# Running the two units of a quad together, array mode by array mode, in a retention and adapter kernel

## The chip, the core and the metric

The kernel runs on one core of one Trainium2 chip. The metric is the device time of one execution in microseconds (us). The profiles were taken by the hardware profiler during one execution.

## What is computed

The reference is a retention layer (attention without a softmax and with an exponential decay) whose output goes through a mixture of eight low-rank adapters, of which each token takes its best two. Everything is float32, with B = 8 sequences, H = 8 heads, S = 576 positions and 64 elements a head.

```python
scores = scale * q @ k.T                       # per sequence and head
Dmat   = where(i >= j, gamma[h] ** (i - j), 0) # causal decay
x      = (scores * Dmat) @ v                   # (8, 8, 576, 64)
x      = x.transpose(0, 2, 1, 3).reshape(4608, 512)
logits = x @ w_gate                            # 8 experts
w      = softmax of the two largest logits
out    = x + sum over the two experts e:  w_e * (x @ A[e]) @ B[e]   # rank 16
```

## The kernel before

Positions are cut into four full chunks of 128 and a last one of 64. A **quad** is one chunk of four sequences; its q, k and v arrive in three loads of 1 MB each. A **unit** is two sequences of a quad, so a quad has two units. There are 16 full units, numbered 0 to 15, and two units of the half chunk, 16 and 17. Quad n holds units 2n and 2n+1. Each unit passes eleven stages. The diff and the prediction call them by their letters:

| stage | engine | what it does | TensorE rows x columns |
|---|---|---|---|
| T | TensorE, then ScalarE or VectorE | transposes q (16 matmuls) and k (16), copies them out of PSUM | 64 x 128 |
| S | TensorE, VectorE | scores, 8 matmuls for each of two sequences, then the mask multiply into rt | 64 x 128 |
| Q | TensorE | state of earlier chunks times q, into px | 64 x 64 |
| U | TensorE, VectorE, GpSimd | state update, k times v, into pu, then P | 128 x 64 |
| R | TensorE, VectorE | rt times v, added into px, then the scaling into xT | 128 x 64 |
| B | TensorE | transposes xT back to tokens, into po | 64 x 128 |
| Z | TensorE, VectorE | x times A and the gate, into pz, then the two best logits | 128 x 128 |
| V | ScalarE | sigmoid of the logit difference | |
| W | VectorE | mixing weights, and zc = z times weight | |
| X | TensorE, ScalarE | transposes zc, copies it to zT | 128 x 128 |
| Y | TensorE, ScalarE | adds zT times B into po, copies po to osb, and a store follows | 128 x 128 |

The column on the right is the part of the array that each matmul of the stage addresses, which follows from the partitions of its operands. This document calls it the array mode. In the half chunk S, Q and R use 64 x 64.

Program order is kept on every engine by hand. The main loop handles one unit a turn:

```python
def issue(n):                      # the loads of quad n, all on the SyncE queue
    tl = [iop.tile([128, QUAD, H, Dh], FP32, tag=tag, name=tag) for tag in ("q32", "k32", "v32")]   # 3 buffers each
    ...
for t in range(NU):
    if units[t][2] == 0:           # first unit of a quad
        issue(quads.index(units[t][:2]) + 2)      # two quads ahead
    ... # (t = 0, 1, 2: a written-out start)
    if is_full(t):
        stage_S(t, (0,))
        stage_V(t - 1)
        stage_T(t + 1, ("qT",))
        stage_S(t, (1,))
        stage_W(t - 1)
        stage_T(t + 1, ("kT",))
        stage_B(t - 1)
        if units[t][0] > 0:
            stage_Q(t)
        ...
        stage_U(t)
        scale_k(t + 1)             # GpSimd scales k in place, U needs it
        ...
        stage_R(t)
        stage_X(t - 1)
        stage_Z(t)
        stage_Y(t - 1)
        continue
    ... # (the half chunk: units 16 and 17, one after the other)
```

PSUM banks come from a list of eight: a stage takes the bank that has been free longest in program order, and gives it back when the copy out of it has been put into the program.

Of the kernel before, what the change touches and what calls it, by code (L numbers as in the profile page):

```python
# [18 lines left out]
def kernel(  # L19
# [180 lines left out]
    def issue(n):  # L200
        if n >= len(quads):
            return
        c, qd = quads[n]
        first = n == 0
        tl = [
            iop.tile([128, QUAD, H, Dh], FP32, tag=tag, name=tag) for tag in ("q32", "k32", "v32")
        ]
        if c == NFULL:
            if qd > 0:
                return  # L210
            for src, dst in zip((q, k, v), tl):
                for g in range(2):
                    nc.sync.dma_start(
                        out=dst[64 * g : 64 * g + 64].rearrange("p s h d -> p (s h) d"),
                        in_=src[HALF * g : HALF * g + HALF, :, C * c : C * c + L, :].rearrange(
                            "s h j d -> j (s h) d"
                        ),
                    )
            for u in range(2):
                nat[(c, u, 0)] = [x[:, 2 * u : 2 * u + 2] for x in tl]  # L220
            return

        def load(n, lo, hi):
            nc.sync.dma_start(
                out=tl[n][:, lo:hi].rearrange("p b h d -> p (b h) d"),
                in_=(q, k, v)[n][
                    QUAD * qd + lo : QUAD * qd + hi, :, C * c : C * c + C, :
                ].rearrange("b h j d -> j (b h) d"),
            )

        if first:
            for lo in (0, 2):
                for n in range(3):
                    if n == 2 and lo == 0:
                        load_A()
                    load(n, lo, lo + 2)
        else:
            for n in range(3):
                load(n, 0, 4)
        for sl in range(2):  # L240
            nat[(c, qd, sl)] = [x[:, 2 * sl : 2 * sl + 2] for x in tl]
# [23 lines left out]
                op=ALU.mult,  # L265
            )

    def stage_T(t, names=("qT", "kT")):

        s = st.setdefault(t, {})  # L270
        for nm in names:
            src = nat[units[t]][0 if nm == "qT" else 1]
            dst = s[nm] = wk.tile([128, 2, HP, C], FP32, tag=nm, name=nm)
            ps = [bank([128, HP, 2, L], f"p{nm}") for _ in range(2)]
            for hp in range(HP):
                for b in range(2):
                    for g in range(2):
                        mm(
                            ps[g][:, hp, b, :],
                            lhsT=src[rows(g), b, 2 * hp : 2 * hp + 2, :],  # L280
                            rhs=id64[rows(g), :],
                            is_transpose=True,
                            start=True,
                            stop=True,
                        )
            for g in range(2):
                if is_full(t):
                    o = dst[:, :, :, rows(g)].rearrange("p b a i -> p a b i")
                else:
                    o = dst[:, g].rearrange("p a (b i) -> p a b i", b=2)  # L290
                if t == 0 and nm == "kT":
                    for b in range(2):
                        x = dst[:, b, :, rows(g)]
                        if g == 1:
                            vec("tensor_copy", out=x, in_=ps[g][:, :, b])
                        else:
                            act("copy", out=x, in_=ps[g][:, :, b])
                elif t < 2 and nm == "qT" or t < 3 and nm == "kT" and g == 1:
                    vec("tensor_copy", out=o, in_=ps[g])
                else:  # L300
                    act("copy", out=o, in_=ps[g])
            done(*ps)
# [99 lines left out]
    def stage_R(t):  # L402
# [5 lines left out]
        if is_full(t):  # L408
            for b in range(2):
                for hp in range(HP):  # L410
                    for ho in range(2):
                        h = 2 * hp + ho
                        mm(
                            px[b][rows(ho ^ b), hp, :],
                            lhsT=v32[:, b, h, :],
                            rhs=rt[(b, ho)][:, hp, :],
                            start=(c == 0 and hp == 0),
                            stop=True,
                            skip_group_check=True,
                        )  # L420
                xt = mo.tile([128, HP, C], FP32, tag="xT", name="xT", bufs=6)
                vec("tensor_tensor", out=xt, in0=px[b], in1=asc[b], op=ALU.mult)
                s["xT"].append(xt)
            done(*px)
            return
# [10 lines left out]
                            skip_group_check=True,  # L436
                        )
        for x in range(2):
            xt = mo.tile([128, HP, C], FP32, tag="xT", name="xT", bufs=6)
            vec("tensor_tensor",   # L440
                out=xt.rearrange("p a (y i) -> p a y i", y=2),
                in0=px[x].rearrange("p a (y i) -> p a y i", y=2),
                in1=asc[x][:, :, 0:L].unsqueeze(2).broadcast_to((128, HP, 2, L)),
                op=ALU.mult,
            )
            s["xT"].append(xt)
# [19 lines left out]

    BOTH = (0, 1)

    def stage_X(t, gs=BOTH):
        s = st[t]  # L470
        n = len(gs)
        pzt = bank([128, n, 128], "pzt", FP16)
        for y, g in enumerate(gs):
            mm(
                pzt[:, y, :], lhsT=s["zc"][g], rhs=ident16,
                is_transpose=True, start=True, stop=True,
            )
        zt = mo.tile([128, n, 128], FP16, tag=f"zT{n}", name="zT")
        act("copy", out=zt, in_=pzt)
        done(pzt)  # L480
        for y, g in enumerate(gs):
            s.setdefault("zT", {})[g] = zt[:, y, :]

    def stage_Z(t, gs=BOTH):
        s = st[t]
# [38 lines left out]
    def stage_W(t, gs=BOTH):  # L524
# [3 lines left out]
            stage_V(t, gs)  # L528
        lg, m8, ns, pz, sg = s.pop(("route", gs))
        cm = mo.tile([128, n, E], FP32, tag=f"cm{n}", name="cm")  # L530
        zc = mo.tile([128, n, ER], FP16, tag=f"zc{n}", name="zc")
        for y in range(n):
            vec(
                "scalar_tensor_tensor",
# [78 lines left out]
    for t in range(NU):  # L613
        if units[t][2] == 0:
            issue(quads.index(units[t][:2]) + 2)
        if t == 0:
# [13 lines left out]
            stage_Q(0)  # L630
            stage_R(0)
            stage_T(1, ("qT",))
            stage_T(1, ("kT",))
            scale_k(1)
            stage_Z(0)
            stage_S(1)
# [3 lines left out]
            stage_R(1)  # L640
            stage_T(2, ("qT",))
            stage_B(0)
            stage_X(0)
            stage_Z(1)
            stage_Y(0, spread=True)
            stage_T(2, ("kT",))
            scale_k(2)
            for ho in range(2):
                gp.tensor_tensor(
                    out=maskh[ho], in0=trih.unsqueeze(1).broadcast_to((128, HP, L)),  # L650
                    in1=heads(1, ho, L), op=ALU.mult,
                )
            continue
        if t == 1:
            continue
        if t == NU - 1:
            break
        if t == 2:
            stage_T(3, ("qT",))
            stage_B(1)  # L660
            stage_V(1)
            stage_S(2)
            stage_W(1)
            stage_T(3, ("kT",))
            stage_U(2)
            stage_Q(2)
            scale_k(3)
            stage_R(2)
            stage_X(1)
            stage_Z(2)  # L670
            stage_Y(1)
            continue
        if is_full(t):
            stage_S(t, (0,))
            stage_V(t - 1)
            stage_T(t + 1, ("qT",))
            stage_S(t, (1,))
            stage_W(t - 1)
            stage_T(t + 1, ("kT",))
            stage_B(t - 1)  # L680
            if units[t][0] > 0:
                stage_Q(t)
            if not is_full(t + 1):
                stage_S(t + 1)
                stage_Q(t + 1)
            stage_U(t)
            scale_k(t + 1)
            if units[t][0] == 0:
                stage_Q(t)
            stage_R(t)  # L690
            stage_X(t - 1)
            stage_Z(t)
            stage_Y(t - 1)
            continue

        stage_W(t - 1)
        stage_T(t + 1)
        stage_B(t - 1)
        stage_R(t)
        stage_Q(t + 1)  # L700
        stage_X(t - 1)
        stage_Z(t)
        stage_W(t)
        stage_Y(t - 1)
        stage_S(t + 1)
        stage_B(t)
        stage_X(t)
        stage_R(t + 1)
        stage_Y(t)
        for g in range(2):  # L710
            stage_Z(t + 1, (g,))
            stage_W(t + 1, (g,))
        stage_B(t + 1)
        for g in range(2):
            stage_X(t + 1, (g,))
            stage_Y(t + 1, (g,), spread=True, last=True)
    return

# [1 line left out]
_INS = ['q', 'k', 'v', 'moe_w_gate', 'moe_A', 'moe_B']  # L720
_OUTS = [((4608, 512), 'float32')]
# [25 lines left out]
```

## Time and profile before

The kernel takes 194.46 us, the median of three runs (193.17 to 195.02). The profiled execution has a span of 191.0 us.

| engine | busy us | share of the span |
|---|---|---|
| TensorE matmuls (PE) | 179.9 | 94% |
| TensorE weight loads (PEld) | 163.3 | 85% |
| VectorE (DVE) | 110.3 | 58% |
| ScalarE (ACT) | 72.1 | 38% |
| GpSimd (POOL) | 58.9 | 31% |

PE time overlaps with PEld time: the weights of one matmul are loaded while the one before runs. A matmul's modelled end runs past the start of the next, so the spacing of starts says more than the busy time. In the timeline each line gives the start, the length, the engine, the source line, the operation, output and inputs, the shapes and the number of instructions merged. A float32 matmul other than a transpose appears as two instructions. The queue of SyncE is SP; the time of a DMA line there is the time that the queue took to accept it, and its data lands later. HBM traffic over the span is 28.91 MB read and 9.44 MB written. All of the loads and nearly all of the stores go through the SyncE queue, in program order.

### The profile page before, as it was taken

The numbers are of one execution on the slowest core, as the hardware profiler recorded it, in microseconds if no ns is written. First come the engines' busy times: TensorE is split into PE (matmuls) and PEld (weight loads), VectorE is DVE, ScalarE is ACT, GpSimd is POOL, SyncE is SP. The second block draws the span as 40 slices with busy tenths as digits, with TensorE's granted clock in tenths as the row PEclk, the third lists the DMA queues.
The fourth block names the chain that finished last, engine by engine and source line by source line (L and its number), as shares of the span: only waits on it lengthen the run. The fifth ranks groups of instructions, "written<-read, shape, count | busy, mean of one in ns | idle before, by whom it ended". The sixth has DMA issues, their size and how long they took to land. (4 is left out here: it accounts for less than half of the span.)

```text
span 191.0 us, 8118 instructions
## 1 busy us (share of the span) xinstructions
PE 179.9 (94%) x3612; PEld 163.3 (85%) x3612; DVE 110.3 (58%) x282; ACT 72.1 (38%) x196; POOL 58.9 (31%) x70
## 2 busy tenths in 40 slices
PE   7899999999999999999999999999999998988870
PEld 2598999899999999999999999999999998977750
DVE  4476947484646474656564747565564646423650
ACT  4111163445344443526170707061625252070540
POOL 8994026040514242424242332415060600200000
PEclk9999999999999999999999999999999999999997
DMA  6999989896899699897879857989982020020343
GB/s 143 263 243 275 276 239 265 250 274 194 237 314 279 192 283 313 256 280 278 219 201 276 255 184 216 307 210 252 216 231 113 6 83 33 3 113 3 113 110 110
DMA packets 53746, 38.73 MB, mean 203 GB/s; under 512 B 27472, under 2 KB 49104, under 8 KB 53712
## 3 DMA queue, kind: packets, MB, share of 16 engines
q1 hardware_dynamic: 52736, 37.75, 70.3%
q8 instruction: 28, 0.46, 1.0%
q10 hardware_dynamic: 832, 0.34, 0.7%
q0 software_dynamic: 144, 0.13, 0.4%
q14 instruction: 6, 0.05, 0.1%
HBM read 28.91 MB, written 9.44 MB: 201 GB/s over the span
## 5 line engine op out<-in xcount | busy, mean ns | idle before, releaser
L261 POOL TENSOR_TENSOR k<-k,pack 128x512 f32<-128x512 f32 x32 | 32.7, 1043 | 78.6 <-PE pkT L81 73.3
L84 DVE TENSOR_TENSOR rt<-ps,mask 128x512 f32<-128x512 f32 x64 | 40.9, 685 | 16.2 <-PE ps L81 16.0
L81 PE MATMUL pz<-AW,xT 128*128 128x136 f32 x288 | 37.4, 283 | 0.2 <-DVE xT L84 0.2
L81 PE MATMUL ps<-qT,kT 64*128 64x128 f32 x512 | 35.7, 281 | 0.6 <-DVE kT L84 0.6
L81 PEld LDWEIGHTS pz<-AW,xT 128*128 128x128 f32 x288 | 34.6, 190 | 0.7 <-DVE xT L84 0.5
L81 PEld LDWEIGHTS ps<-qT,kT 64*128 64x128 f32 x512 | 31.0, 188 | 3.7 <-PE po L81 2.7
L87 ACT COPY osb<-po 128x256 f32<-128x256 f32 x68 | 20.6, 385 | 28.6 <-PE po L81 26.4
L81 PE MATMUL px<-rt,v 128*64 128x128 f32 x512 | 30.7, 273 | 0.0
L84 DVE TENSOR_TENSOR xT<-px,asc 128x512 f32<-128x512 f32 x36 | 24.6, 690 | 7.7 <-PE px L81 6.6
L81 PEld LDWEIGHTS px<-rt,v 128*64 128x64 f32 x512 | 27.7, 137 | 0.0
L87 ACT COPY zT<-pzt 128x256 f16<-128x256 f16 (+1 forms) x19 | 6.9, 361 | 52.7 <-PE pzt L81 52.7
L400 POOL TENSOR_TENSOR P<-pn,gdec 128x512 f32<-128x512 f32 x12 | 15.3, 1276 | 27.4 <-DVE pn L84 25.9
L87 ACT COPY kT<-pkT 128x512 f32<-128x512 f32 (+1 forms) x34 | 18.0, 580 | 14.1 <-PE pkT L81 14.0
L87 ACT COPY qT<-pqT 128x512 f32<-128x512 f32 x32 | 17.3, 593 | 8.1 <-PE pqT L81 8.1
L84 DVE COPY lg<-pz 128x16 f32<-128x16 f32 (+1 forms) x19 | 3.3, 173 | 26.8 <-PE pz L81 26.8
L81 PE MATMUL pu<-v,k 128*64 128x64 f32 x512 | 18.4, 225 | 0.0
L81 PEld LDWEIGHTS pu<-v,k 128*64 128x64 f32 x512 | 16.2, 138 | 2.3 <-issue 1.9
L81 PE MATMUL px<-qT,P 64*64 64x128 f32 (+1 forms) x512 | 16.1, 261 | 1.6 <-issue 1.6
L84 DVE TENSOR_TENSOR pn<-pu,P 128x512 f32<-128x512 f32 x12 | 8.3, 692 | 15.4 <-PE pu L81 15.4
L81 PEld LDWEIGHTS px<-qT,P 64*64 64x64 f32 x512 | 12.7, 133 | 2.7 <-issue 1.9
L81 PE MATMUL po<-id,xT 64*128 64x64 f32 x288 | 12.6, 224 | 1.1 <-DVE zc L84 1.1
L81 PE MATMUL pkT<-id,k 64*128 64x64 f32 x288 | 12.2, 223 | 0.3 <-DMA k<-in_k_dram 0.3
(51 smaller groups left out, 149.6 us busy)
## 6 DMA issues: line engine op xcount, KB each, us to landing
out_dram<-osb SPq DMA_DIRECT2D x32, 256.0 KB, 4.1
q<-in_q_dram SPq DMA_DIRECT2D x4, 512.0 KB, 6.5
k<-in_k_dram SPq DMA_DIRECT2D x4, 512.0 KB, 6.7
v<-in_v_dram SPq DMA_DIRECT2D x4, 512.0 KB, 7.1
out_dram<-osb SPq DMA_DIRECT2D x6, 128.0 KB, 2.3
Arow<-in_moe_A_dram SPq DMA_DIRECT2D x1, 256.0 KB, 5.1
out_dram<-osb ACTq DMA_DIRECT2D x2, 128.0 KB, 2.7
Bcat<-in_moe_B_dram POOLq DMA_DIRECT2D x1, 128.0 KB, 4.7
```

The costliest lines, as they stand in the source:

```text
L81: chain("pe", nc.tensor.matmul(*args, **kw))
L84: chain("dve", getattr(nc.vector, fn)(**kw))
L87: chain("act", getattr(nc.scalar, fn)(**kw))
L261: gp.tensor_tensor(out=kk[:, b], in0=kk[:, b], in1=gv[:, 0].unsqueeze(2).broadcast_to((128, H, Dh)), op=ALU.mult,)
L400: nc.gpsimd.tensor_tensor(out=Pt, in0=pn, in1=gdec, op=ALU.mult)
```

## The change

The change handles a whole quad a turn, so that stages with the same array mode stand together for both units. Its purpose is to switch the mode less often. Five things come with it:

1. The loop turns once a quad. Scores of units t and t+1 alternate with the transposes of units t+2 and t+3, the next quad. B, X and Y lag behind by four units, Z by two.
2. One transposed copy zT serves both units of a quad (stage X takes a list of units).
3. The buffers follow: two for q (before three), three each for k and v, four for qT, eight for xT (before six), four for zc, two for zT.
4. The start is rewritten: units 2 and 3 run S, U and R before the adapter stages of unit 1 are over, and the transposes of units 4 to 7 stand at the end of a turn, not inside the scores.
5. The two units of the half chunk are placed among the adapter stages of units 12 to 15.

The core of the diff, with cuts marked:

```diff
-            iop.tile([128, QUAD, H, Dh], FP32, tag=tag, name=tag) for tag in ("q32", "k32", "v32")
+            iop.tile([128, QUAD, H, Dh], FP32, tag=tag, name=tag, bufs=n)
+            for tag, n in (("q32", 2), ("k32", 3), ("v32", 3))
...
+        before, near = [u for u in (t - 4, t - 3) if u > 0], (t - 2, t - 1)
+        here = (t, t + 1)
+        for u in here:
+            for b, nm in enumerate(("qT", "kT")):
+                stage_S(u, (b,))
+                if t > 4:
+                    stage_T(u + 2, (nm,))
+            if t > 4:
+                scale_k(u + 2)
+        for u in before:
+            stage_B(u)
+        stage_X(before)
+        stage_Z(near[0])
+        stage_V(near[0])
+        for u in before:
+            stage_Y(u)
+        stage_Z(near[1])
+        stage_V(near[1])
+        if units[t][0] > 0:
+            for u in here:
+                stage_Q(u)
+        for u in near:
+            stage_W(u)
+        for u in here:
+            stage_U(u)
...
+            stage_R(u)
+        if t == 4:
+            for nm in ("kT", "qT"):
+                stage_T(6, (nm,), shared=True)
+            scale_k(6)
+            stage_T(7)
+            scale_k(7)
... (start: after T of unit 2)
+            stage_T(3)
+            scale_k(2)
+            scale_k(3)
+            stage_S(2)
+            stage_W(1)
+            stage_S(3)
+            for u in (2, 3):
+                stage_U(u)
+                stage_Q(u)
+                stage_R(u)
+            for nm in ("kT", "qT"):
+                stage_T(4, (nm,), shared=True)
+            scale_k(4)
+            stage_T(5)
... (end: h = 16, n = 17; the order is)
+    S(16) Q(16) B(12) B(13) X(12,13) Z(14) V(14) Y(12) Y(13) W(14) R(16) S(17) Z(15) V(15) Q(17)
+    W(15) B(14) B(15) X(14,15) Z(16) V(16) Y(14) W(16) R(17) B(16) Y(15) X(16) Z(17) first half
+    V(17) Y(16) Z(17) second half W(17) B(17) X(17) Y(17)
```

The last three lines stand for 47 of the diff, with `stage_` left out.

More of the change, by code (lines that the diff above doesn't have):

```diff
@@ L266, in scale_k, with stage_T @@
             )
-    def stage_T(t, names=("qT", "kT")):
+    def stage_T(t, names=("qT", "kT"), shared=False):
         s = st.setdefault(t, {})
@@ L272, in stage_T @@
             src = nat[units[t]][0 if nm == "qT" else 1]
-            dst = s[nm] = wk.tile([128, 2, HP, C], FP32, tag=nm, name=nm)
+            dst = s[nm] = wk.tile([128, 2, HP, C], FP32, tag=nm, name=nm, bufs=4 if nm == "qT" else 2)
             ps = [bank([128, HP, 2, L], f"p{nm}") for _ in range(2)]
@@ L297, in stage_T @@
                             act("copy", out=x, in_=ps[g][:, :, b])
-                elif t < 2 and nm == "qT" or t < 3 and nm == "kT" and g == 1:
+                elif t < 2 and nm == "qT" or shared and g == 1:
                     vec("tensor_copy", out=o, in_=ps[g])
@@ L420, in stage_R @@
                         )
-                xt = mo.tile([128, HP, C], FP32, tag="xT", name="xT", bufs=6)
+                xt = mo.tile([128, HP, C], FP32, tag="xT", name="xT", bufs=8)
                 vec("tensor_tensor", out=xt, in0=px[b], in1=asc[b], op=ALU.mult)
@@ L438, in stage_R @@
         for x in range(2):
-            xt = mo.tile([128, HP, C], FP32, tag="xT", name="xT", bufs=6)
+            xt = mo.tile([128, HP, C], FP32, tag="xT", name="xT", bufs=8)
             vec("tensor_tensor",
@@ L467, with stage_X @@
     BOTH = (0, 1)
-    def stage_X(t, gs=BOTH):
-        s = st[t]
-        n = len(gs)
+    def stage_X(ts, gs=BOTH):
+        todo = [(t, g) for t in ts for g in gs]
+        n = len(todo)
         pzt = bank([128, n, 128], "pzt", FP16)
-        for y, g in enumerate(gs):
+        for y, (t, g) in enumerate(todo):
             mm(
-                pzt[:, y, :], lhsT=s["zc"][g], rhs=ident16,
+                pzt[:, y, :], lhsT=st[t]["zc"][g], rhs=ident16,
                 is_transpose=True, start=True, stop=True,
             )
-        zt = mo.tile([128, n, 128], FP16, tag=f"zT{n}", name="zT")
+        zt = mo.tile([128, n, 128], FP16, tag=f"zT{n}", name="zT", bufs=2)
         act("copy", out=zt, in_=pzt)
         done(pzt)
-        for y, g in enumerate(gs):
-            s.setdefault("zT", {})[g] = zt[:, y, :]
+        for y, (t, g) in enumerate(todo):
+            st[t].setdefault("zT", {})[g] = zt[:, y, :]
     def stage_Z(t, gs=BOTH):
@@ L530, in stage_W @@
         cm = mo.tile([128, n, E], FP32, tag=f"cm{n}", name="cm")
-        zc = mo.tile([128, n, ER], FP16, tag=f"zc{n}", name="zc")
+        zc = mo.tile([128, n, ER], FP16, tag=f"zc{n}", name="zc", bufs=4)
         for y in range(n):
@@ L632 @@
             stage_T(1, ("qT",))
-            stage_T(1, ("kT",))
+            stage_T(1, ("kT",), shared=True)
             scale_k(1)
@@ L642 @@
             stage_B(0)
-            stage_X(0)
+            stage_X([0])
             stage_Z(1)
+            stage_V(1)
             stage_Y(0, spread=True)
-            stage_T(2, ("kT",))
+            stage_T(2, ("kT",), shared=True)
+            stage_T(3)
             scale_k(2)
+            scale_k(3)
[10 more added lines that the diff above has]
+            stage_T(5)
+            scale_k(5)
             for ho in range(2):
@@ L653 @@
             continue
-        if t == 1:
+        if t < 4 or units[t][2] or not is_full(t):
             continue
[L656 to L687, printed above, removed]
-            if units[t][0] == 0:
[L689 to L716, printed above, removed]
@@ L717 @@
-    return
+        before, near = [u for u in (t - 4, t - 3) if u > 0], (t - 2, t - 1)
[14 more added lines that the diff above has]
+            stage_Y(u)
@@ new lines @@
+        stage_Z(near[1])
[7 more added lines that the diff above has]
+            stage_U(u)
+            if units[t][0] == 0:
+                stage_Q(u)
+            stage_R(u)
[5 more added lines that the diff above has]
+            scale_k(7)
+    h, n = NU - 2, NU - 1
@@ new lines @@
+    stage_S(h)
+    stage_Q(h)
+    stage_B(h - 4)
+    stage_B(h - 3)
+    stage_X([h - 4, h - 3])
+    stage_Z(h - 2)
+    stage_V(h - 2)
+    stage_Y(h - 4, spread=True)
+    stage_Y(h - 3, spread=True)
+    stage_W(h - 2)
+    stage_R(h)
+    stage_S(n)
+    stage_Z(h - 1)
+    stage_V(h - 1)
+    stage_Q(n)
+    stage_W(h - 1)
+    stage_B(h - 2)
+    stage_B(h - 1)
+    stage_X([h - 2, h - 1])
+    stage_Z(h)
+    stage_V(h)
+    stage_Y(h - 2)
+    stage_W(h)
+    stage_R(n)
+    stage_B(h)
@@ L720 @@
+    stage_Y(h - 1, spread=True)
+    stage_X([h])
+    stage_Z(n, (0,))
+    stage_V(n, (0,))
+    stage_Y(h, spread=True)
+    stage_Z(n, (1,))
+    for g in range(2):
+        stage_W(n, (g,))
+    stage_B(n)
+    for g in range(2):
+        stage_X([n], (g,))
+        stage_Y(n, (g,), spread=True, last=True)
 _INS = ['q', 'k', 'v', 'moe_w_gate', 'moe_A', 'moe_B']
```

## The prediction

> **What bounds the kernel now.** I read the page's shares first, then TensorE's timeline in a turn of the loop, then the waits, then the SyncE queue. The page says that TensorE is busy nearly throughout, and that the DMA row stays near full for three quarters of the span:
>
> ```profile
> PE 179.9 (94%) x3612; PEld 163.3 (85%) x3612; DVE 110.3 (58%) x282; ACT 72.1 (38%) x196; POOL 58.9 (31%) x70
> ...
> PEclk9999999999999999999999999999999999999997
> DMA  6999989896899699897879857989982020020343
> ```
>
> One turn, from scores to scores, in TensorE's timeline:
>
> ```profile
> 95.25 1.16 PE L81 MATMUL ps<-qT,kT 64*128 64x128 f32 x16
> 96.25 0.66 PE L81 MATMUL pqT<-id,q 64*128 64x64 f32 x16
> 96.74 1.11 PE L81 MATMUL ps<-qT,kT 64*128 64x128 f32 x16
> 97.69 0.65 PE L81 MATMUL pkT<-id,k 64*128 64x64 f32 x16
> 98.18 0.67 PE L81 MATMUL po<-id,xT 64*128 64x64 f32 x16
> 98.78 1.10 PE L81 MATMUL px<-qT,P 64*64 64x128 f32 x32
> 99.81 1.15 PE L81 MATMUL pu<-v,k 128*64 128x64 f32 x32
> 100.79 1.92 PE L81 MATMUL px<-rt,v 128*64 128x128 f32 x32
> 102.64 0.29 PE L81 MATMUL pzt<-ident,zc 128*128 128x128 f16 x2
> 102.77 2.07 PE L81 MATMUL pz<-AW,xT 128*128 128x136 f32 x16
> 104.67 0.60 PE L81 MATMUL po<-Bcat,zT 128*128 128x256 f16 x4
> 105.20 1.16 PE L81 MATMUL ps<-qT,kT 64*128 64x128 f32 x16
> ```
>
> No line names a releaser, and each block starts before the one above it ends. TensorE sets the pace at 9.95 us a unit (105.20 - 95.25), repeated from 45 to 155 us. Differences of starts show the mode switches. B, 16 transposes, gives way to Q after 0.60, while the like block of qT gives way to scores of its own mode after 0.49: 0.11 more. The first scores, after Y, take 1.00 and the second, after transposes, 0.95: 0.05 that a switch leaves in the block behind it. So I take **0.16 us a switch**, four to a unit (64x128 to 64x64, to 128x64, to 128x128, and back). VectorE's busy time in this turn is 5.88 us, ScalarE's 4.11 and GpSimd's 3.32: none is near 9.95.
>
> The waits of TensorE after 154 us are small ones, in the half chunk:
>
> ```profile
> PE px L81 <- issue: 1.6, 2, 0.8
> PE po L81 <- DVE zc L84: 1.1, 2, 0.9
> PE po L81 <- ACT zT L87: 1.1, 2, 0.7
> ```
>
> Then the queue of SyncE, early on (quad 3, four stores, quad 4):
>
> ```profile
> 40.10 1.26 SPq L224 DMA_DIRECT2D q<-in_q_dram  x1
> 41.82 5.63 SPq L224 DMA_DIRECT2D k<-in_k_dram  x1
> 47.91 3.32 SPq L224 DMA_DIRECT2D v<-in_v_dram  x1
> 51.33 5.69 SPq L579 DMA_DIRECT2D out_dram<-osb  x4
> 57.23 0.71 SPq L224 DMA_DIRECT2D q<-in_q_dram  x1
> 58.40 5.13 SPq L224 DMA_DIRECT2D k<-in_k_dram  x1
> ```
>
> SyncE is still handing out quads 3 and 4 at 40 to 60 us although their loop turns have come: it is never ahead of the memory, it is paced by it. From 8 to 57 us the windows give a DMA share of 0.93 at 256 GB/s. The queries by line add the landings: 1 MB of k of quad 2 lands 9.1 us after its issue (37.0), v of quad 3 9.3 us after (57.2), k of quad 4 10.6 us after (69.0). TensorE needs quad 4 in this kernel only for the transposes of unit 8, at 76.34, so the loads are hidden.
>
> **What the Trainium skill says.** "TensorEngine Tiling (Array Packing)", Key Properties: changing the tiling mode, not only the tile, drains TensorE. The trace agrees, with the 0.16 us above. "Perfetto Trace Analysis", Identifying the Most-Contended Engine: matmul busy share is a poor measure and the weight loads' is better. Here it is 85%, and the gap to 100% holds the switches. "DMA: Bandwidth & Descriptors", Issuing engines are not separate DMA queues: all transfers share 16 DMA engines, so no other queue would bring more bandwidth. The 0.93 share agrees. "TensorE: Matmul & The Clock Gate", Part 1, What's actually happening: about 3.4 us of idleness halves the clock. No run here shows it, since PEclk stays at 9; it matters for rival 1.
>
> **Switches removed.** I counted them in the order of the built programs: 75 before, 50 after, and a turn of two units goes from eight to four. The number of matmuls in each stage stays the same. 25 x 0.16 = **4.0 us** less, all of it on TensorE, which sets the end.
>
> **Work moved within the loop.** A turn should take 2 x 9.95 - 4 x 0.16 = 19.26, say 19.3 us. Would VectorE, ScalarE or PSUM stop it? Scores of one sequence and the transposes behind them take 0.95 + 0.49 = 1.44 on TensorE; the two masks follow one another at 0.60 in this trace, so VectorE needs 1.2, and the two copies of a transpose 2 x 0.48 = 0.96 on ScalarE. With eight banks in rotation B reuses those of the third score block, read long before. The eight osb copies of two Y (8 x 0.265 = 2.1 us) end before U takes those banks, about 4 us after Y. I find no new wait here. The joined zT copy removes about eight copies of 0.37 from ScalarE, which is 38% busy: nothing.
>
> **The start: earlier need for data.** This is what I expect to cost. Up to T of unit 2 at 26.73 the order is unchanged. After that, in blocks from the turn above: T(2), T(3) to 28.3, about 0.4 waiting for ScalarE, S(2), S(3) 3.8, U and R of both 2 x 2.8, to 38.0 with one switch; T(4) needs k of quad 2, landed at 37.0, in time. T(4), T(5) to 40.1; S(4), S(5), B(1), X(1), Z(2), Y(1), Z(3) to 49.0; two Q, two U, two R to 56.4; T(6), T(7) need quad 3, landed by 52.8, and end at 58.5. The next turn's S(6) then meets the q transpose of unit 8 at 59.5 and its k transpose at 60.9. That is 17 us earlier than before, and this is quad 4. In the new program quad 4 follows quad 3 in the queue with no stores between. A load of 1 MB lands 4.05 us after the last in the unmixed stretch (quads 1 and 2 land at that pace), and v of quad 3 lands at 57.2 as before. So q of quad 4 lands at 61.2, k at 65.3. TensorE waits 1.7 and then 2.7: **4.4 us lost**. Each later quad has a whole turn's lead: 3 MB of loads at 4.05 and 1 MB of stores (four of them landed within 2.5) take about 12.2 + 2.5 = 14.7 us of the 19.3. K of quad 5 would land near 79, and T(10) asks after 83. One stall, then, in one turn.
>
> **The end.** The turn with k of quad 4 sets the clock. T(8) of k at 65.3, the rest of the turn 17.0, so the turn of quad 4 starts at 82.3; four turns of 19.3 bring 159.5. What remains is 20.4 us of blocks (the half-chunk blocks of 64 matmul instructions at 1.0 to 1.1 from this trace), 13 switches or 2.0, and waits. In place of 5.5 us of waits now I take 3 to 4: two "issue" gaps of 0.80, which go with long rows of 64x64 matmuls that remain, and the last chain Z, V, W, X, zT, Y of unit 17, which stays. TensorE ends at 159.5 + 25.9 = 185.4, before at 186.4. The stores behind it are alike, 4.6 us.
>
> **Sum.** Switches -4.0, waits in the start and end -1.5, quad 4 +4.4: -1.1 us. The time is 194.46 - 1.1 = **193.3 us**.
>
> **Rivals.** 1. *DMA eats the gain entirely.* For it: the 0.93 share and the slow patch after 43 us, where quad 3 took 6 us for q instead of 4. Were quad 4 to land 3 us later, or a long wait to slow the clock, the time would be 196 to 198. 2. *The data comes in time.* For it: the stores that sit ahead of quad 4 today are gone, and the DMA moved 300 GB/s in some windows. Then only the switches count and the time is 188.5 to 190. Against it: 256 GB/s over a long stretch is with the queue never empty. 3. *VectorE becomes the bound in the back-to-back scores* of units 2 to 5, eight masks of 0.60 against 3.8 us of TensorE. U and R follow with 5.6 us in which it catches up, so at most 0.5 us; and time lost before T(8) only shortens the wait for quad 4.
>
> **Range and chances.** The landing of quad 4 is good to about 2 us either way, the tail to 1.5, the switches to 1. The three times of before lie 1.85 us apart, so the median adds some 0.9. I take 190.4 to 196.5. Over 2% faster means below 190.6, which takes rival 2 nearly whole: 0.15. Over 2% slower, above 198.4, takes rival 1 at its worst: 0.04. Within 2%: 0.81.
>
> **What would show it.** Right: turns of about 19.3 us with four switches; one wait on the k and q loads of 3 to 5 us near 60; no others in the loop; the last turn ending near 159. Wrong: a wait for VectorE or ScalarE repeated in every turn; a switch that costs much more or less than 0.16 once modes are grouped; quad 4 landing before 61; load waits in later turns.

## The result and the profile after

The changed kernel takes 189.78 us against 194.19 us, as medians. The ratio is 0.9715 (95% interval 0.9635 to 0.9794). Ratios in this document leave out the slow executions, which run over 1.5% longer than the fastest of the same kernel, while medians hold all of them. Two later comparisons on other chips gave 0.9802 (0.9754 to 0.9850) and 0.9824 (0.9757 to 0.9890). So it is some 2 to 3% faster, and the two later intervals reach down to 1.5 and 1.1%. The prediction of 193.3 us stood for 0.994, and the measured time lies 0.6 us below its range of 190.4 to 196.5.

The profile read here is that of the repeat (experiment 1), with a span of 187.7 us. Its page, in the rows that were shown of the kernel before:

```profile
PE 175.9 (94%) x3612; PEld 163.3 (87%) x3612; DVE 114.7 (61%) x294; ACT 66.0 (35%) x177; POOL 59.2 (32%) x70
...
PE   7898999999999499999999999999999999999970
...
PEclk9999999999999999999999999999999999999995
DMA  6998899999799997999597779999920050033175
```

TensorE is still the bound, with 4.0 us less of busy time. One digit stands out: the 4 in the row of PE, at about 63 us. TensorE's timeline shows what it is. This is the whole turn of quad 3 (units 6 and 7, with the transposes of quad 4 between their scores):

```profile
59.68 1.16 PE L81 MATMUL ps<-qT,kT 64*128 64x128 f32 x16
61.61 0.71 PE L81 MATMUL pqT<-id,q 64*128 64x64 f32 x16 [0.77 <-DMA q<-in_q_dram]
62.13 1.14 PE L81 MATMUL ps<-qT,kT 64*128 64x128 f32 x16
65.40 0.72 PE L81 MATMUL pkT<-id,k 64*128 64x64 f32 x16 [2.13 <-DMA k<-in_k_dram]
65.92 1.14 PE L81 MATMUL ps<-qT,kT 64*128 64x128 f32 x16
...
68.81 1.19 PE L81 MATMUL po<-id,xT 64*128 64x64 f32 x32
69.93 0.40 PE L81 MATMUL pzt<-ident,zc 128*128 128x128 f16 x4
70.16 2.07 PE L81 MATMUL pz<-AW,xT 128*128 128x136 f32 x16
72.07 1.04 PE L81 MATMUL po<-Bcat,zT 128*128 128x256 f16 x8
72.95 2.02 PE L81 MATMUL pz<-AW,xT 128*128 128x136 f32 x16
74.90 1.98 PE L81 MATMUL px<-qT,P 64*64 64x128 f32 x64
76.80 1.15 PE L81 MATMUL pu<-v,k 128*64 128x64 f32 x32
...
82.31 1.16 PE L81 MATMUL ps<-qT,kT 64*128 64x128 f32 x16
```

The brackets hold the two load waits, 0.77 and 2.13 us. The profile names no wait in the lines below them. Both units now pass each mode together: 32 transposes of B in a row, 8 matmuls of Y, 64 instructions of Q. This turn takes 22.63 us (82.31 - 59.68). The windows of the four turns after it, with the length and the busy us of each engine:

```profile
82.31:101.61 19.30, 19.30 (x398) 18.66 (x396) 11.78 (x30) 8.04 (x21) 6.66 (x7) 1.00 0.88 271
101.61:120.91 19.30, 19.30 (x398) 18.66 (x396) 11.78 (x30) 8.04 (x21) 6.66 (x7) 1.00 0.84 245
120.91:140.21 19.30, 19.30 (x398) 18.66 (x396) 11.78 (x30) 8.05 (x21) 6.66 (x7) 1.00 0.85 202
140.21:159.51 19.30, 19.30 (x398) 18.66 (x396) 11.78 (x30) 8.04 (x21) 2.56 (x3) 1.00 0.16 58
```

Each is 19.30 us, where two turns of the kernel before took 19.90. No other engine comes near: VectorE is busy for 11.78. From 159.51 TensorE needs 23.6 us to its last block's end at 183.1. The waits of that stretch, 1.4 us, all stand in the last three microseconds, in the chain of unit 17:

```profile
PE po L81 <- ACT zT L87: 0.9, 2, 0.5
PE pzt L81 <- DVE zc L84: 0.5, 1, 0.5
```

### The profile page after: what moved, and what is told of

Read it like the earlier page. It is cut to its first block, busy times and chain, and to the rows that moved or that the text cites. A ratio compares the mean times of both kernels' runs of the same rounds, so it can differ in the third digit from the quotient of the medians.

```text
span 192.1 us, 8116 instructions
## 1 busy us (share of the span) xinstructions
PE 178.7 (93%) x3612; PEld 165.9 (86%) x3612; DVE 114.5 (60%) x294; ACT 66.0 (34%) x177; POOL 59.0 (31%) x70
## 5 line engine op out<-in xcount | busy, mean ns | idle before, releaser
L81 PEld LDWEIGHTS ps<-qT,kT 64*128 64x128 f32 x512 | 32.4, 196 | 1.9 <-issue 0.8
L87 ACT COPY qT<-pqT 128x512 f32<-128x512 f32 x30 | 16.1, 593 | 42.2 <-PE pqT L81 42.2
L87 ACT COPY kT<-pkT 128x512 f32<-128x512 f32 (+1 forms) x32 | 17.1, 582 | 31.0 <-PE pkT L81 19.6
L87 ACT ACTIVATE sg<-lg,ns 128x8 f32<-128x8 f32 x36 | 9.0, 293 | 26.7 <-DVE ns L84 26.4
L87 ACT COPY osb<-po 128x256 f32<-128x256 f32 x60 | 17.5, 386 | 1.7 <-PE po L81 1.0
L81 PE MATMUL pqT<-id,q 64*128 64x64 f32 x288 | 12.7, 234 | 3.6 <-DMA q<-in_q_dram 3.6
L81 PEld LDWEIGHTS pqT<-id,q 64*128 64x128 f32 x288 | 11.7, 148 | 4.9 <-issue 4.9
L81 PE MATMUL pkT<-id,k 64*128 64x64 f32 x288 | 12.9, 229 | 1.7 <-DMA k<-in_k_dram 1.6
L81 PE MATMUL px<-qT,P 64*64 64x128 f32 (+1 forms) x512 | 14.1, 259 | 0.0
L81 PEld LDWEIGHTS pkT<-id,k 64*128 64x128 f32 x288 | 11.4, 143 | 3.1 <-issue 2.6
```

The source lines that it names most:

```text
L81: chain("pe", nc.tensor.matmul(*args, **kw))
L87: chain("act", getattr(nc.scalar, fn)(**kw))
```

## Experiments

"The changed kernel" below is always the one measured on the same chip in the same set, unless another is named.

**1. The changed kernel again.** No edit.

> The changed kernel, run again and timed beside the others. The first profile of it lost 7.9 us in the turn of quad 4 (27.2 us against 19.3 for the later turns): 5.2 us of waits for the loads of q and k, and the rest on a TensorE clock of 0.5 that followed a wait of 3.6 us. Theory A (the wait for quad 4 is there in every execution, with a length that varies): time 187 to 190 us, and the profile again shows load waits between 59 and 68 us, 2 to 5 us in sum. Rival B (the wait belongs to that one execution; an ordinary one has the data in time): no load wait after 40 us in the profile, and the turn of quad 4 takes 19.3 us.

Measured: 190.48 us, ratio 0.9802. The lines above are its profile. The loads are waited for again, 2.9 us in sum. The first profile, of an execution of 193.77 us, has 5.2 us, and that of the third measurement, under 9 to 12 below, has 3.3. So the wait is no accident of one execution, and rival B falls. Its length varies, and experiment 7 shows on what else it depends.

**2. One load moved.** v of quad 3 goes behind k of quad 4. It isn't needed before U of unit 6, at 76.80 in the repeat.

```diff
-            for n in range(3):
-                load(n, 0, 4)
+            load(0, 0, 4)
+            load(1, 0, 4)
+            while late:
+                late.pop()()
+            if (c, qd) == (1, 1):                 # quad 3
+                late.append(lambda: load(2, 0, 4))
+            else:
+                load(2, 0, 4)
```

> Only the order of loads changes: v of quad 3 (1 MB, needed only by U and R of units 6 and 7, after 70 us) is put behind k of quad 4. Theory A: q and k of quad 4 land about 4 us earlier, the load wait falls to under 1 us and the clock stays up; 2 to 3 us faster than the changed kernel, 185.5 to 187.5 us. Rival B: as fast as the changed kernel within 0.5 us.

Measured: 186.82 us, ratio to before 0.9614 (0.9569 to 0.9658), 3.7 us less than the changed kernel. The same stretch of TensorE's timeline:

```profile
60.97 1.16 PE L81 MATMUL ps<-qT,kT 64*128 64x128 f32 x16
61.94 0.69 PE L81 MATMUL pqT<-id,q 64*128 64x64 f32 x16
62.43 1.15 PE L81 MATMUL ps<-qT,kT 64*128 64x128 f32 x16
63.37 0.69 PE L81 MATMUL pkT<-id,k 64*128 64x64 f32 x16
```

No bracket is left: both transposes start as soon as TensorE gets to them. The same bytes in another order take the wait away. Another wait, of 1.40 us for k of quad 2, stands at 40 us in this profile and not in that of the repeat.

**3. The transposes moved, not the load.** Units 8 and 9 are transposed at the end of the turn, as units 6 and 7 are.

```diff
-                if t > 4:
+                if t > 6:
                     stage_T(u + 2, (nm,))
...
-        if t == 4:
+        if t in (4, 6):
             for nm in ("kT", "qT"):
-                stage_T(6, (nm,), shared=True)
+                stage_T(t + 2, (nm,), shared=True)
```

> The transposes of units 8 and 9 move from between the scores of units 6 and 7 to the end of that turn, some 17 us later, as units 6 and 7 have it already. Nothing else changes, 50 mode switches stay 50. Theory A: no load wait near 60 us any more, 2 to 3.5 us faster than the changed kernel, 185 to 187 us. Rival B: no change, or up to 0.5 us slower, because four score blocks then run back to back (3.8 us of TensorE against 4.8 us of masks on VectorE).

Measured: 187.04 us, ratio 0.9616 (0.9573 to 0.9658), which is 3.6 us less than the changed kernel by the ratios. The four score blocks back to back cost nothing that the waits show. Two different cures, one of the supply and one of the demand, bring the same amount, so the wait for quad 4 cost the changed kernel about 3.5 us. The profile of the repeat shows 2.9 of them. Where the rest comes from isn't shown; the last section has a candidate, a clock that falls after such a wait in some executions.

**4. Part of the grouping undone.** Q of the second unit stands between R of the first and U of the second.

```diff
-        if units[t][0] > 0:
-            for u in here:
-                stage_Q(u)
         for u in near:
             stage_W(u)
         for u in here:
+            stage_Q(u)
             stage_U(u)
-            if units[t][0] == 0:
-                stage_Q(u)
             stage_R(u)
```

> One part of the grouping is undone: Q of the second unit stands between R of the first and U of the second, so each of six turns has two more mode switches; 62 instead of 50 in all, with the same matmuls. Theory A (a switch costs 0.16 us on TensorE): the turns in which no load is waited for take 19.6 instead of 19.3 us, 1.9 us slower in all than the changed kernel. Rival C (the gain does not come from the mode switches but from the new end and from waits): turns of 19.3 us and the same time.

Measured: 192.55 us, 2.1 us slower than the changed kernel by the medians. By the ratios, 0.9880 (0.9828 to 0.9933) against 0.9802, it is 1.5 us. Its end of a turn, in TensorE's timeline, and two undisturbed turns in its windows:

```profile
117.37 1.15 PE L81 MATMUL pu<-v,k 128*64 128x64 f32 x32
118.35 1.92 PE L81 MATMUL px<-rt,v 128*64 128x128 f32 x32
120.20 1.10 PE L81 MATMUL px<-qT,P 64*64 64x128 f32 x32
121.24 1.15 PE L81 MATMUL pu<-v,k 128*64 128x64 f32 x32
```

```profile
84.49:104.10 19.61, 19.61 (x399) 18.62 (x397) 11.78 (x30) 8.04 (x21) 6.65 (x7) 1.00 0.87 271
...
124.07:143.67 19.60, 19.60 (x398) 18.62 (x397) 11.78 (x30) 8.04 (x21) 6.65 (x7) 1.00 0.80 190
```

The same matmuls take 0.30 to 0.31 us longer for two more switches, which makes 0.155 us each. This is the cleaner figure. The 1.5 us for 12 of them make 0.13, but the total holds other differences as well: this profile waits 2.22 us for k of unit 1, that of the repeat 0.82. Rival C falls as the whole explanation.

**5. The new end undone.** B, X and Y of units 12 to 15 come ahead of the half chunk as far as possible. This is not the end of the kernel before, which also ran its units one by one. The order of the stages behind the last turn:

```
B12 B13 X12,13 Z14 V14 Y12 Y13 Z15 V15 W14 W15 B14 B15 S16 Q16 X14,15 Y14 Y15 R16
Q17 Z16 V16 S17 W16 B16 X16 R17 Y16 Z17 V17 W17 B17 X17 Y17
```

> Part 5 of the change is undone as far as it can be: B, X, Y of units 12 to 15 come first, in one row, and the two units of the half chunk follow behind them and among themselves, with 51 mode switches against 50. In the changed kernel TensorE takes 23.8 us from the last turn to its end, of which 1.4 are waits. Theory A (the new end is worth what the waits of the old one cost): waits for zc, zT or xT of 2 to 4 us in sum return, 1.5 to 3 us slower than the changed kernel. Rival D (the end is bound by its matmuls, and interleaving brings nothing): within 0.5 us.

Measured: 193.04 us with a ratio of 0.9946 (0.9914 to 0.9979), where experiment 7 on the same chip, which has the new end, has 189.61 and 0.9808. By the ratios that is 2.7 us. In the trace the end takes 26.6 us (161.60 to 188.2) against 23.6. The waits of TensorE after 160 us:

```profile
PE pzt L81 <- DVE zc L84: 1.7, 2, 1.2
PE po L81 <- ACT zT L87: 1.5, 3, 0.7
PE px L81 <- issue: 0.3, 1, 0.3
PE pz L81 <- DVE xT L84: 0.3, 1, 0.3
```

They sum to 3.8 us against 1.4 with the new end. ("issue" stands for a wait for which the profile shows no cause.) The first two, 3.2 us, belong to the routing chain of a unit (Z, V, W, X, zT, Y), with too little beside it. Rival D falls.

**6. A long row of short matmuls put back.** Q of unit 17 directly behind S of unit 17.

```diff
     stage_S(n)
+    stage_Q(n)
     stage_Z(h - 1)
     stage_V(h - 1)
-    stage_Q(n)
```

> At the end of the changed kernel Q of unit 17 moves directly behind S of unit 17, so that R(16), S(17), Q(17) make one row of 3 x 64 instructions in mode 64 x 64; two switches fewer. In the kernel before, two such rows showed gaps of 0.80 and 0.84 us in which TensorE waited for nothing that the profile shows, and the changed kernel shows none. Theory E (such a gap comes when a long row of short matmuls uses up the instructions that were fetched ahead): a gap named issue of 0.5 to 1 us appears in this row. Rival F (the gaps belonged to something else in the old order): no such gap, and the end is 0.3 us shorter.

Measured in one execution, so only the waits are read. First the two gaps of the kernel before, then this row in TensorE's timeline:

```profile
162.50 0.27 PE L81 MATMUL px<-qT,P 64*64 64x64 f32 x2 [0.80 <-issue]
...
170.98 1.16 PE L81 MATMUL px<-rh,v 64*64 64x64 f32 x64
171.96 0.99 PE L81 MATMUL px<-qT,P 64*64 64x64 f32 x55
173.80 0.35 PE L81 MATMUL px<-qT,P 64*64 64x64 f32 x9 [0.84 <-issue]
```

```profile
167.22 1.16 PE L81 MATMUL px<-rh,v 64*64 64x64 f32 x64
168.20 1.16 PE L81 MATMUL pe<-qT,kT 64*64 64x64 f32 x61
...
169.21 0.85 PE L81 MATMUL px<-qT,P 64*64 64x64 f32 x42
171.04 0.57 PE L81 MATMUL px<-qT,P 64*64 64x64 f32 x21 [0.98 <-issue]
```

The gap is back. After some 170 of the 192 short instructions TensorE stands still for 0.98 us, and the profile shows nothing that it waits for.

**7. Separate zT copies.** Stage X for each unit by itself.

> Part 2 of the change is undone: each unit has its own zT tile and copy again (stage X per unit), everything else as in the changed kernel. Theory A (ScalarE is not on the path): the same turns of 19.3 us and the same time within 0.5 us. Rival G (the copies hold up Y): turns longer by 0.1 to 0.3 us and waits for zT.

Measured: 189.61 us, ratio 0.9808 (0.9775 to 0.9840), the same as the changed kernel's 0.9802 on another chip. Rival G's waits did appear, twice 0.4 us at Z in the end, but no difference shows in the time. The joined copy isn't where the gain comes from.

This profile also tells something of the wait for quad 4. The order of the loads is that of the changed kernel, yet nothing near 60 us waits:

```profile
17.04 0.71 PE L81 MATMUL pkT<-id,k 64*128 64x64 f32 x16 [1.65 <-DMA k<-in_k_dram]
...
61.81 1.16 PE L81 MATMUL ps<-qT,kT 64*128 64x128 f32 x16
...
64.23 0.71 PE L81 MATMUL pkT<-id,k 64*128 64x64 f32 x16
```

This execution lost its time at the start, waiting 1.65 us for k of unit 1, and came to the scores of unit 6 at 61.81 instead of 59.68. Its q and k of quad 4 landed just in time, and the turn took 19.3 us. So an execution that loses time early waits less for quad 4, and the two losses don't add up.

**8. The same row cut, in the kernel before.** Q of unit 16 goes behind R of unit 15.

```diff
             if not is_full(t + 1):
                 stage_S(t + 1)
-                stage_Q(t + 1)
             stage_U(t)
...
             stage_R(t)
+            if not is_full(t + 1):
+                stage_Q(t + 1)
```

> The kernel before with one move: Q of unit 16 goes behind R of unit 15, so that the row Q(15), S(16), Q(16) of mode 64 x 64 is cut in two by U and R; one switch more. Theory E: the gap of 0.80 us named issue near 162 us is gone, the second one near 173 stays. Rival F: a gap of about 0.8 us stays at this place. From one look, only the waits in the profile tell, not the time.

Measured in one execution. In place of the row Q(15), S(16), Q(16), 160 instructions long, there are now shorter ones, and they run through. The later row still has its gap, of 0.65 us:

```profile
159.98 1.35 PE L81 MATMUL pe<-qT,kT 64*64 64x64 f32 x64
...
164.09 1.16 PE L81 MATMUL px<-qT,P 64*64 64x64 f32 x64
...
173.24 0.38 PE L81 MATMUL px<-qT,P 64*64 64x64 f32 x9 [0.65 <-issue]
```

So in one execution each, cutting the row removed the gap and joining one made it. The length of the row doesn't decide alone: the later row has only 128 instructions, as in the kernel before, and its gap comes after 119 of them. Experiment 5 has a gap of 0.33 us after 123 of 128. The repeat ran two rows of 128 through. That the gap is TensorE running out of fetched instructions remains a reading: a further one of 0.36 us stood in an R block of this same profile, at 102 us, and one of 0.66 us among the transposes of B in the third profile of the changed kernel, at 109 us, where no row of 64 x 64 matmuls is.

**9 to 12. A better version.** The changed kernel once more, then the two cures with one more move: in the start the q transposes of units 4 and 5 come ahead of their k transposes.

```diff
-            for nm in ("kT", "qT"):
-                stage_T(4, (nm,), shared=True)
-            scale_k(4)
-            stage_T(5)
+            stage_T(4, ("qT",), shared=True)
+            stage_T(5, ("qT",))
+            stage_T(4, ("kT",), shared=True)
+            scale_k(4)
+            stage_T(5, ("kT",))
```

> The changed kernel once more, as the measure for the three versions beside it. 189 to 190.5 us, and in the profile one turn, that of quad 4, longer than the others by 2 to 5 us through waits for loads.

> v of quad 3 is loaded behind k of quad 4, and in the start the q transposes of units 4 and 5 stand ahead of the k transposes, so that k of quad 2 is asked for 1 us later (it was waited for by 1.4 us in the version with the loads alone). Theory A (early loads are what is left of the DMA's cost): no load wait over 0.5 us after 30 us, 3.5 to 4.5 us faster than the changed kernel, 185.5 to 186.5 us. Rival B: as fast as the changed kernel.

> The transposes of units 8 and 9 at the end of the turn of quad 3, and the same q-first order in the start. Theory A: 3 to 4 us faster than the changed kernel, 185.5 to 187 us. The two cures meet the same wait, so neither should beat the other by more than 1 us.

> Both cures and the q-first order together. Theory A (one wait, two cures): no faster than the better of the two by more than 0.3 us. If the loads still cost something in other turns, it would be 1 us faster or more.

| kernel | us | ratio to before, 95% interval |
|---|---|---|
| changed kernel | 190.41 | 0.9824 (0.9757 to 0.9890) |
| load moved, q first | 187.58 | 0.9662 (0.9612 to 0.9712) |
| transposes late, q first | 187.48 | 0.9660 (0.9610 to 0.9710) |
| both, q first | 188.57 | 0.9681 (0.9617 to 0.9746) |

The three can't be told apart, nor from experiments 2 and 3, which did without q first. So that move brought nothing that can be measured: in the profile of the load moved with q first, the wait of 1.40 us that it was meant for is gone, and one of 0.6 us for the copy of kT has come. The expected 3.5 to 4.5 us of the second were about 3. Both cures together bring no more than one, as expected of two cures for one wait. Experiments 2 and 3 do as well as any, 3.8% below the kernel before.

## Why the prediction missed

- **Switches: right.** Expected 0.16 us each and turns of 19.3. Measured 0.155 in the turns (0.13 by the totals) and 19.30. The Trainium skill, "TensorEngine Tiling (Array Packing)", Key Properties, says that a change of mode drains TensorE. The turns of experiment 4 show the price of a change; what happens inside TensorE they don't show.
- **VectorE, ScalarE and PSUM: right.** No wait for them inside a turn.
- **The earlier need for quad 4: right.** Expected were landings at 61.2 and 65.3. In the repeat q was issued at 51.91 and landed 9.6 us later, at 61.5, and k was issued at 56.35 and landed 8.9 us later, at 65.3. The next turn was to start at 82.3 and started at 82.31, and the last one was to end near 159.5 and ended at 159.51. That it fits to the tenth is luck: in the first profile q was there only at 63.90 and k at 67.59, and in experiment 4 k at 67.14. The waits were 2.9 us and not 4.4, because the start had lost more than 1 us elsewhere (0.8 of it waiting for k of unit 1), which only shortened the wait, as the prediction says under its third rival. Experiments 2 and 3 put the cost at 3.6 to 3.7 us of the time.
- **The end: the step that failed.** The prediction took 20.4 us of blocks, 2.0 of switches and "3 to 4" of waits, 25.9 in all to TensorE's end. The end took 23.6. Blocks and switches fit: 23.6 less 1.4 of waits is 22.2. The waits were mis-sized by about 2 us. The prediction kept "two 'issue' gaps of 0.80, which go with long rows of 64x64 matmuls that remain". None of them is in the end of any of the three profiles of the changed kernel, and that is 1.6 of the 2 us. The new order puts another mode after 128 short instructions at most. Experiments 6 and 8 fit this as the reason, but rows of 128 have had such gaps too, so why both are gone stays open in part. The 5.5 us that the prediction took for the waits of the old end doesn't come out of its own lines either: these sum to 3.8, and with one of 0.2 that it leaves out to 4.0. Experiment 5 shows that without the interleaving the end takes about 3 us more.
- **The sum.** On the profiles it was to be -1.0 us at TensorE's end (186.4 to 185.4); with 183.1 it is -3.3. Of the 2.3 us of difference the end accounts for all. The times differ by more, by 3.4 to 5.5 us in the three ratios, and what lies beyond 3.3 no experiment here assigns.
- **The rivals.** The measured 189.78 lies where rival 2 ("the data comes in time") put it, 188.5 to 190. Yet rival 2 was wrong: the data came late, and the end made up for it. A time that fits is no proof of its mechanism. Rival 1 came about in part in the first profile: quad 4 landed over 2 us late and the clock fell to half, but that execution took 193.77 us and not 196 to 198. Rival 3 didn't come about: no profile shows a wait for a mask.

The account of the 3.3 us between the two profiles is then: 25 switches -3.9, waits of the end -2.6 (4.0 in the kernel before, 1.4 now), the wait for quad 4 +2.9, and a later start of +1.0 (k of unit 2 is transposed at 27.72 instead of 26.73, before the first change of order). They sum to -2.6, so 0.7 us isn't assigned.

## What to carry over

Count the switches of the array mode in program order: here grouping like modes gained about their number times the price of one, 0.155 us, where the new order brought no new waits. Any regrouping moves the need for data: compare the new time of need with the landing of each load, since a load that was hidden can turn into the largest wait, and one moved load can give it back. And go through the end of a kernel wait by wait, not as a lump: here its waits decided whether the prediction held.

## What the runs showed that was not expected

A wait of TensorE can cost more than its length. In the first profile the wait for q of quad 4 lasted 3.60 us, and its turn took 27.2 us, 7.9 more than the later ones, of which the waits are 5.2. In experiment 6 the wait for k lasted 3.88. Windows of 2 us in experiment 6; the last three columns are the granted clock, the DMA share and GB/s:

```profile
60.00:62.00 2.00, 1.38 (x30) 1.18 (x26) 1.85 (x4) 1.47 (x3) 1.39 (x2) 1.00 1.09 326
62.00:64.00 2.00, 0.00 (x0) 0.00 (x0) 0.66 (x2) 0.00 (x0) 0.00 (x0) 1.00 0.15 45
64.00:66.00 2.00, 0.75 (x20) 0.78 (x22) 0.00 (x0) 0.00 (x0) 0.00 (x0) 1.00 0.69 160
66.00:68.00 2.00, 2.00 (x34) 2.00 (x34) 0.77 (x2) 1.07 (x2) 1.97 (x2) 0.61 1.12 351
68.00:70.00 2.00, 2.00 (x27) 2.00 (x27) 0.62 (x2) 1.07 (x2) 0.08 (x1) 0.54 0.86 299
70.00:72.00 2.00, 2.00 (x54) 1.93 (x51) 1.18 (x2) 1.19 (x3) 1.56 (x2) 1.00 0.95 270
```

The clock falls to about half after the wait. If it is just half there, 0.61 and 0.54 over 2 us each make some 3.4 us of it. The Trainium skill, "TensorE: Matmul & The Clock Gate", Part 1, gives about 3.4 us of idleness as what halves the clock, and the prediction had named it as a danger. Both waits are longer than that and agree with it. Shorter ones do not: in experiment 7 the clock was 0.66 and 0.50 from 18 to 22 us, after a wait of 1.65 us. In experiment 5 it was 0.60 and 0.55 from 66 to 70 us, after waits of 1.00 and 2.12 us, while in the repeat, with 0.77 and 2.13 us, it stayed at 1.00. So waits of about 2 us brought it in some executions and not in others, and what decides isn't shown. In experiment 7 it cost about 1.6 us: from the late transpose of k to the scores of unit 2 it took 14.73 us (17.04 to 31.77), in the repeat 13.12 (16.51 to 29.63).

The second surprise is the line from 62 to 64 us. TensorE waits for a load there, and the DMA moves 45 GB/s at a share of 0.15. The loads are late although the DMA engines are nearly idle. In the same stretch the SyncE queue of this experiment shows one line that takes long:

```profile
53.85 3.73 SPq L225 DMA_DIRECT2D k<-in_k_dram  x1
58.04 5.50 SPq L225 DMA_DIRECT2D v<-in_v_dram  x1
```

The queue takes 5.50 us to accept v, against 3.73 for k. In the first profile it takes 5.77 us for k of quad 4 itself, with 94 and 90 GB/s from 60 to 64 us. The kernel before had such a line too (5.63 us, at 41.82), with 138 GB/s from 45 to 50 us. The prediction took that stretch for a slow memory ("it is paced by it"), but low rates at a low DMA share speak against that. What holds the queue up was not tried.
